# Two of four token tiles written in the output's order ahead of a feed-forward layer, their rows normalised there, and every result stored straight to the output

## The chip, the cores and the metric

The kernel runs on one core of one Trainium2 chip. The metric is device time of one execution in microseconds (us); a kernel's time is the median of its runs. The engines named below are TensorE (PE in the profile, PEld for its weight loads), VectorE (DVE), ScalarE (ACT), GpSimd (POOL) and SyncE (SP), whose queue issues the DMA transfers of this kernel.

## The reference

Eight batches, each of 448 tokens with 12 heads of 64 (768 channels), go through attention, a two-dimensional Fourier transform of which the real part is kept, a layer norm and a feed-forward layer.

```
q_n, k_n = rmsnorm(q, g_q), rmsnorm(k, g_k)
attn = softmax(q_n @ k_n^T / 8) @ v                # [8, 12, 448, 64]
x    = attn as [8, 448, 768]
u    = x + real(fft(fft(x, tokens), channels))
un   = (u - mean(u)) / sqrt(var(u) + 1e-6)
out  = u + relu(un @ w1) @ w2                      # 768 -> 3072 -> 768
```

All of it is wanted in fp32 accuracy. The kernel gets it by splitting each operand of a product into a high and a low part and multiplying in three passes.

## The kernel before, in words

**Stages.** For each batch there are two streams of work. `aux(b)` does the attention and the spectral part and ends in four token tiles: tiles of 113, 112, 111 and 112 rows (`LENS`) with 768 channels. Tiles 0 and 1 hold the first 225 tokens in descending order (they read `xT[:, :, 222 + t :: -2]`), tiles 2 and 3 (`mirror`) the rest. `ffn(b)` does the feed-forward layer of one batch: `up(m)` (18 matmuls, L866) makes one of 24 blocks of 128 hidden channels, `down(g, d)` (12 matmuls, L887) adds a group of four hidden blocks to one of six blocks `acc[:, d]` of output channels. Batch 0's `aux` runs first, with part of batch 1's; after that the driver merges `ffn(b)` with `aux(b+1)`, step by step in proportion to their costs, so that the last token tiles of `aux(b+1)` fall into the end of `ffn(b)`. The order of the instructions on each engine is then set by a scheduler that works on the merged list, and a change of one instruction can move its neighbours. The order of SP's DMA issues is set in the same way, and one that has to wait holds up those behind it.

**A token tile** (`token_tile`, L558 to L609). PE transposes x into PSUM (L578); two operations on DVE add the Fourier part, giving `u` and its row sums in `st`. SP stores `u` to a scratch in DRAM, `u_dram` (L591), from where it comes back later as the residual. DVE makes minus the mean from the row sums; ACT makes `un = u - mean` (Identity with a bias) and then squares `un` **into u**, with the row sums kept. This square overwrites `u`, so it waits until the L591 store has been read and has landed. DVE turns the sum into variance plus epsilon, GpSimd raises it to the power -1/2, and that is `rstd`. In the kernel before nothing ahead of the feed-forward layer uses `rstd`: since relu(r x) = r relu(x) for r > 0, the rows are scaled only at the output. In the profile the helpers' operations all carry L113.

**The feed-forward's input** (`ffn_input`, L773 to L789). For each of six blocks of 128 channels PE transposes the four tiles' pieces into one PSUM tile (24 transposes, L778); ACT copies it to `unT`'s high part and DVE subtracts to get the low part, 128 x 448 each.

**Weights.** They are converted in batch 0 (GpSimd, ACT and DVE; loads at L667, results to DRAM at L716) and afterwards loaded from there, once for each batch: a load is issued (L726) as soon as a matmul group has freed a buffer. w1 comes in tiles of 768 KB, w2 in tiles of 512 KB, three buffers each.

**The output** (`output_half` L823 to L841, `store` L804 to L819). The residual of a tile is loaded from `u_dram` (L828; rows of 113 and 111 go in two pieces), PE transposes three blocks of `acc` (L832), and DVE makes `rstd * product + residual`. A tile 2 or 3 is stored straight to every second row of the output (L819). For tiles 0 and 1, whose rows stand in descending order, the result is first stored to the scratch (L809) and then copied DRAM to DRAM with the rows reversed (L810), in pieces of 48 channels (192 bytes); token 224 goes by itself (L815). The output of batch b is done in the first `up` steps of batch b+1. In the last batch it is done in two halves of 384 channels, the second at the very end, with pieces of 24 channels.

## Time and profile before

| | |
|---|---|
| time, median of 3 runs | 2231.12 us (2229.54 to 2231.13) |
| span of the profiled execution | 2227.2 us |
| time of the profiled execution beyond its span | not given; the span is 3.9 us below the median |
| TensorE busy | 2092.4 us, 94% of the span |
| VectorE, ScalarE, GpSimd busy | 72%, 48%, 24% |
| feed-forward of batch 0 begins | 194.6 us |
| first residual load of batch 0's output | 517.4 us |

Rows of the profile are read as follows. A row of the timeline gives the start in us from the span's start, the duration, engine, line, operation and tiles (out<-in), a count when several like instructions are merged, and in brackets how long the engine had been idle and what released it. `SPq` rows are DMA issues: their duration is that of the issue, not that of the transfer, and where a row merges several (x3) it reaches from the first to the end of the last. A DMA row of the form "x1, 512.0 KB, 5.7" gives the issues in a window, their size and the median time from issue to landing. The windows view gives, for each stretch, its length, the busy time of PE, PEld, DVE, ACT and POOL with counts, the TensorE clock granted, the mean busy share of the DMA engines and GB/s. The view of one tile lists the forms of its operations with least, median and longest duration in ns.

### The profile page before, as it was taken

How to read it: one execution, taken by the hardware profiler on the slowest of the kernel's cores; microseconds unless marked ns; L12 is line 12 of the kernel's file. 1: busy time of each engine (PE TensorE's matmuls, PEld its weight loads, DVE VectorE, ACT ScalarE, POOL GpSimd, SP SyncE). 2: the span in 40 equal slices, each digit the busy share in tenths (PEclk: the TensorE clock that was granted, in tenths of full speed). 3: DMA queues.
4: the chain of work that ended last, by engine and by line, in shares of the span. 5: the costliest groups of instructions: out<-in, count | busy, mean ns of one | idle time of the engine just before them, and what ended most of it. 6: DMA issues, size and time to landing. Idle time of an engine off the chain costs nothing.

```text
span 2227.2 us, 31403 instructions
## 1 busy us (share of the span) xinstructions
PE 2092.4 (94%) x11164; PEld 1847.3 (83%) x11164; DVE 1612.1 (72%) x3083; ACT 1060.8 (48%) x2290; POOL 536.6 (24%) x322
## 2 busy tenths in 40 slices
PE   6877978779999999999999999999999999999997
PEld 3336867668999999999999999999999999998996
DVE  7897889788788587866787587867787687763122
ACT  6866766545554355524554355524554355422100
POOL 5773567644121021111211021101221022000000
PEclk8988988889999999999999999999999999999999
DMA  5555565658656675557655675558556674549665
GB/s 155 160 172 199 188 192 192 233 197 271 192 169 183 201 215 167 177 178 230 185 168 178 207 216 168 173 173 240 179 166 182 201 224 152 181 136 280 213 209 137
DMA packets 298238, 425.32 MB, mean 191 GB/s; under 512 B 186545, under 2 KB 224418, under 8 KB 298082
## 3 DMA queue, kind: packets, MB, share of 16 engines
q1 hardware_dynamic: 298082, 423.32, 61.1%
q8 instruction: 89, 1.46, 0.3%
q14 instruction: 67, 0.55, 0.1%
HBM read 363.47 MB, written 65.27 MB: 193 GB/s over the span
## 4 chain that ended last, share of the span: by engine, by line
PE 77%; DVE 10%; DMA 4%; ACT 4%; issue 2%; POOL 2%; SPq 0%; DVEq 0%; POOLq 0%; ACTq 0%
PE h L866 29%; PE o L887 27%; PE S L357 6%; PE av L443 4%; PE pt L431 4%; DMA dblw<-w 2%; PE y L546 1%; PE qk L320 1%; POOL magw L684 1%; DVE mn L113 1%; ACT P L113 1%; DMA w<-w 1%; DVE sm L113 1%; DVE eo L113 1%; PE oT L832 1%
## 5 line engine op out<-in xcount | busy, mean ns | idle before, releaser
L887 PE MATMUL o<-hs,w 128*128 128x448 f32 x3456 | 795.9, 371 | 11.5 <-DMA w<-w 4.4
L866 PE MATMUL h<-unT,w 128*128 128x448 f32 x3456 | 787.5, 373 | 7.5 <-ACT w L685 6.3
L866 PEld LDWEIGHTS h<-unT,w 128*128 128x128 f32 x3456 | 646.7, 190 | 61.3 <-ACT w L685 7.1
L887 PEld LDWEIGHTS o<-hs,w 128*128 128x128 f32 x3456 | 639.4, 189 | 68.1 <-issue 6.0
L113 ACT ACTIVATE P<-S,mn 112x448 f32<-112x448 f32 x384 | 243.3, 635 | 222.2 <-DVE mn L113 211.4
L113 DVE TENSOR_REDUCE mn<-S 112x1 f32<-112x448 f32 x384 | 233.7, 618 | 47.0 <-PE S L357 43.9
L113 POOL TENSOR_TENSOR qkn<-raw 112x1024 f32<-112x1024 f32 x47 | 90.3, 1922 | 719.7 <-PE qk L320 493.5
L113 ACT ACTIVATE hs<-h 128x448 fp32r<-128x448 f32 x192 | 104.4, 544 | 295.4 <-PE h L866 294.3
L113 DVE TENSOR_TENSOR acc<-o,acc 128x448 f32<-128x448 f32 x240 | 149.0, 621 | 109.8 <-PE o L887 108.5
L113 DVE SCALAR_TENSOR_TENSOR hs<-h,hs 128x448 fp32r<-128x448 f32 x192 | 119.2, 621 | 126.6 <-ACT hs L113 124.6
L113 ACT CAST T<-pt 128x448 fp32r<-128x448 f32 x252 | 133.0, 533 | 136.4 <-PE pt L431 134.2
L443 PE MATMUL av<-T,vhl 128*128 128x448 f32 x504 | 178.9, 387 | 13.2 <-DVE T L113 9.6
L113 DVE TENSOR_TENSOR T<-pt,T 128x448 fp32r<-128x448 f32 x252 | 154.9, 618 | 27.9 <-ACT T L113 26.2
L113 POOL TENSOR_TENSOR ss<-ss,nhalf 112x16 f32<-112x16 f32 x48 | 147.5, 3074 | 110.4 <-DVE ss L113 107.9
L113 DVE TENSOR_SCALAR P<-P,sm 112x448 f32<-112x448 f32 x336 | 164.9, 525 | 4.7
L431 PE MATMUL pt<-ident,P 112*128 112x112 f32 x1008 | 146.6, 263 | 8.2 <-ACT P L113 4.3
L357 PE MATMUL S<-KD,QT 128*112 128x448 f32 x352 | 138.8, 396 | 9.3 <-ACT P L113 4.8
L431 PEld LDWEIGHTS pt<-ident,P 112*128 112x128 f32 x1008 | 122.8, 143 | 28.6 <-ACT P L113 4.7
L113 POOL TENSOR_TENSOR rstd<-st,nhalf 112x1 f32<-112x1 f32 (+2 forms) x32 | 18.3, 572 | 494.8 <-DVE st L113 487.4
L357 PE MATMUL S<-rounded,QT 128*112 128x448 f32 x352 | 132.2, 377 | 1.7 <-DVE rounded L113 1.6
L443 PEld LDWEIGHTS av<-T,vhl 128*128 128x128 f32 x504 | 95.5, 190 | 24.7 <-DVE T L113 11.4
L113 DVE TENSOR_SCALAR sm<-sm 112x2 f32<-112x2 f32 x192 | 60.3, 314 | 59.0 <-ACT P L113 56.6
(122 smaller groups left out, 2598.8 us busy)
## 6 DMA issues: line engine op xcount, KB each, us to landing
w<-w SPq DMA_DIRECT2D x288, 512.0 KB, 4.4
w<-w SPq DMA_DIRECT2D x192, 768.0 KB, 4.6
dblw<-w SPq DMA_DIRECT2D x30, 512.0 KB, 4.3
dblw<-w SPq DMA_DIRECT2D x16, 768.0 KB, 4.4
raw<-q SPq DMA_DIRECT2D x96, 112.0 KB, 4.5
raw<-k SPq DMA_DIRECT2D x96, 112.0 KB, 3.4
v<-v SPq DMA_DIRECT2D x96, 96.0 KB, 3.5
u_dram<-u SPq DMA_DIRECT2D x24, 336.0 KB, 3.2
```

What stands on the lines that cost most here:

```text
L113: ins = emit(*args, **kwargs)
L320: nc.tensor.transpose(pt[:, c * C : (c + 1) * C], qk[:, i, c].rearrange("t h d -> t (h d)"), ident[:C, :C],)
L357: ins = nc.tensor.matmul(s_, QT[:, h, cs], K[:, h], start=step == 0, stop=step == 1)
L431: nc.tensor.transpose(pt[:, c * C : (c + 1) * C], Pc[c][:, 512 * h + j * 128 : 512 * h + (j + 1) * 128], ident[:C, :C],)
L443: nc.tensor.matmul(av[:, :S], lv, T[:, i], start=(j == 0 and i == 0), stop=False)
L546: nc.tensor.matmul(o, src[:, par, t0 : t0 + n], D1[:, ri, par, cols], start=i != 1, stop=i != 0,)
L684: behind(nc.gpsimd.tensor_tensor(out=bits, in0=bits, in1=low, op=ALU.add))
L832: nc.tensor.transpose(op[:n, j * 128 : (j + 1) * 128], accs[b][:, 3 * half + j, t0 : t0 + n], ident,)
L866: pace(nc.tensor.matmul(o, w[:, a, c], unT[c][:, z], start=n == 0, stop=n == 17))
L887: pace(nc.tensor.matmul(o, w[:, a, f], hs[4 * g + f][:, z], start=n == 0, stop=n == 11))
```

## The change

Four edits belong together:

- In `token_tile`, the tiles 0 and 1 get a further DMA behind the L591 store: a copy DRAM to DRAM with reversed rows from `u_dram` to a new scratch `u_turned` (L593), in pieces of 48 channels.
- The norm is finished there: ACT squares `u` with the bias directly (its result goes to `un`'s place and is not used), DVE and GpSimd make the reciprocal deviation, one more DVE operation makes the bias times it, and ACT writes the fully scaled `un`. `rstd` and its use at the output are gone.
- `ffn_input` writes the first 225 columns of each `unT` in reversed order: the copy by ACT and the subtraction by DVE are made in two pieces (225 and 223 columns), six more operations on each of the two engines for each batch.
- At the output the residual of tiles 0 and 1 is loaded from `u_turned`, DVE's operation is a plain addition, and all results are stored directly (L824, and L820 for token 224). The scratch store and the copy behind it (L809, L810) are gone: 18 of each before, against 16 copies at L593 now.

```diff
+TURNED = (N2, 0, NT, NT + N1 - 2)
...
             for r in rows_of(n):
                 nc.sync.dma_start(u_dram[b % 2, i4, r], u[r])
+            if not mirror:
+                nc.sync.dma_start(
+                    u_turned[b % 2, t, :n].rearrange("t (c d) -> c t d", c=16),
+                    u_dram[b % 2, t, n - 1 :: -1].rearrange(
+                        "t (c d) -> c t d", c=16
+                    ),
+                )
...
-            A.activation(un, u, AF.Identity, bias=st[:n, 2:3])
-            A.activation(u, un, AF.Square, accum_out=st[:n, 3:4])
-            rstd = sb.tile([N1, 1], F32, tag="rstd", name=f"rstd{b}_{i4}", bufs=8)
+            A.activation(un, u, AF.Square, bias=st[:n, 2:3], accum_out=st[:n, 3:4])
             V.tensor_scalar(
                 out=st[:n, 3:4], in0=st[:n, 3:4], scalar1=1.0 / DM, scalar2=EPS,
                 op0=ALU.mult, op1=ALU.add,
             )
             G.tensor_tensor(
-                out=rstd[:n], in0=st[:n, 3:4], in1=nhalf[:n, :1], op=ALU.pow
-            )
...
+                out=st[:n, 3:4], in0=st[:n, 3:4], in1=nhalf[:n, :1], op=ALU.pow
+            )
+            V.tensor_tensor(
+                out=st[:n, 2:3], in0=st[:n, 2:3], in1=st[:n, 3:4], op=ALU.mult
+            )
+            A.activation(
+                un, u, AF.Identity, bias=st[:n, 2:3], scale=st[:n, 3:4]
+            )
...
-            A.copy(t[:, 0], pt[:, :S])
-            sub(t[:, 1], pt[:, :S], t[:, 0])
+            for to, src in (
+                (t[:, :, :NT], pt[:, NT - 1 :: -1]), (t[:, :, NT:], pt[:, NT:S])
+            ):
+                A.copy(to[:, 0], src)
+                sub(to[:, 1], src, to[:, 0])
...
-        if i < 2:
-            turned = u_dram[b % 2, i]
-            nc.sync.dma_start(turned[:N2, cols], u[:N2, cols])
-            nc.sync.dma_start(
-                out[b, i : i + 223 : 2, cols].rearrange("t (c d) -> c t d", c=16),
-                turned[N2 - 1 :: -1, cols].rearrange("t (c d) -> c t d", c=16),
-            )
-            if i == 0:
-                nc.sync.dma_start(out[b, 224:225, cols], u[N2:n, cols])
...
+        if i == 0:
+            nc.sync.dma_start(out[b, 224:225, cols], u[:1, cols])
+            u, n = u[1:], n - 1
+        rows = out[b, i : i + 2 * n - 1 : 2] if i < 2 else out[b, 228 - i : S : 2]
+        for r in rows_of(n):
+            nc.sync.dma_start(rows[r, cols], u[r, cols])
...
+            kept = (u_turned if i < 2 else u_dram)[b % 2, i]
             for r in rows_of(n):
-                nc.sync.dma_start(residual[i][r], u_dram[b % 2, i, r])
+                nc.sync.dma_start(residual[i][r], kept[r])
...
-        V.scalar_tensor_tensor(
-            out=uh, in0=op[:n, :384], scalar=rstds[b, i][:n], in1=uh,
-            op0=ALU.mult, op1=ALU.add,
-        )
+        add(uh, op[:n, :384], uh)
```

SP's queue at the end of batch 2's feed-forward, where the last token tiles of batch 3 are made, reads as follows before the change. `u_1` and `u_3` are the odd token tiles, `w_105` to `w_107` w2 tiles of 512 KB, and `ur_0` is the residual of batch 2's tile 0.

```order
L726 DMA w_105_9706<-w_5_108 128x1024
L591 DMA u_dram<-u_1_9530 112x768
L726 DMA w_106_9722<-w_5_108 128x1024
L591 DMA u_dram<-u_3_9552 112x768
L828 DMA ur_0_9837<-u_dram 112x768
L828 DMA ur_0_9837<-u_dram 1x768
L726 DMA w_107_9738<-w_5_108 128x1024
```

The same place after the change:

```order
L735 DMA w_105_9747<-w_5_109 128x1024
L591 DMA u_dram<-u_1_9570 112x768
L735 DMA w_106_9763<-w_5_109 128x1024
L593 DMA u_turned<-u_dram 16x112x48
L591 DMA u_dram<-u_3_9593 112x768
L834 DMA ur_0_9890<-u_turned 112x768
L834 DMA ur_0_9890<-u_turned 1x768
L735 DMA w_107_9779<-w_5_109 128x1024
```

The reversed copy of tile 1 now stands between the weight load `w_106` and the store of `u_3`, ahead of the weight load `w_107`; it reads what the `u_1` store two places before it writes. The pattern is the same in each of the five transitions to batches 2 to 6.

On DVE, at the same place of the program, the two operations that make `u_1` stand among the reductions of the attention (`mn`, the row extremes of the scores) and the additions to `acc`. Before:

```order
L113 TENSOR_REDUCE mn_0_0_9878<-S_0_0_0_9880 112x1
L113 SCALAR_TENSOR_TENSOR u_1_9530,st_1_9531<-x_100_9534,smdf_1_9511 112x384
L113 SCALAR_TENSOR_TENSOR u_1_9530,st_1_9531<-x_101_9539,smdf_1_9511 112x384
L113 TENSOR_REDUCE mn_0_0_9878<-S_0_0_1_9881 112x1
L113 TENSOR_TENSOR acc_7236<-o_5_0_9692,acc_7236 128x448
```

After:

```order
L114 TENSOR_REDUCE mn_0_0_9930<-S_0_0_0_9932 112x1
L114 TENSOR_REDUCE mn_0_0_9930<-S_0_0_1_9933 112x1
L114 SCALAR_TENSOR_TENSOR u_1_9570,st_1_9571<-x_100_9574,smdf_1_9551 112x384
L114 SCALAR_TENSOR_TENSOR u_1_9570,st_1_9571<-x_101_9579,smdf_1_9551 112x384
L114 TENSOR_TENSOR acc_7277<-o_5_0_9733,acc_7277 128x448
```

The second reduction has moved ahead of `u_1`.

At the end of the program SP's queue holds the second half of the last batch's results. Its last eight transfers before the change:

```order
L809 DMA u_dram<-ur_0_21335 112x384
L815 DMA out_dram<-ur_0_21335 1x384
L809 DMA u_dram<-ur_1_21346 112x384
L819 DMA out_dram<-ur_3_21365 112x384
L810 DMA out_dram<-u_dram 16x112x24
L819 DMA out_dram<-ur_2_21355 96x384
L810 DMA out_dram<-u_dram 16x112x24
L819 DMA out_dram<-ur_2_21355 15x384
```

And its last six after it:

```order
L824 DMA out_dram<-ur_0_21434 112x384
L824 DMA out_dram<-ur_1_21444 112x384
L824 DMA out_dram<-ur_2_21452 96x384
L824 DMA out_dram<-ur_3_21462 112x384
L824 DMA out_dram<-ur_2_21452 15x384
L820 DMA out_dram<-ur_0_21434 1x384
```

The two stores to the scratch and the two copies that read it are replaced by two direct stores.

More of the change, by code (lines that the diff above doesn't have):

```diff
@@ L185, in spectral_block @@
     u_dram = dram.tile([2, 4, N1, DM], F32, name="u_dram")
+    u_turned = dram.tile([2, 2, N1, DM], F32, name="u_turned")
     def load_gains():
@@ L485, in attention @@
             yield 0
-    rstds = {}
     halves = {}
@@ L604, in token_tile @@
             G.tensor_tensor(
-                out=rstd[:n], in0=st[:n, 3:4], in1=nhalf[:n, :1], op=ALU.pow
+                out=st[:n, 3:4], in0=st[:n, 3:4], in1=nhalf[:n, :1], op=ALU.pow
             )
-            rstds[b, i4] = rstd
-            u = un
-            uns[i4] = u
+            V.tensor_tensor(
[4 more added lines that the diff above has]
+            )
+            uns[i4] = un
         for t in range(2):
@@ L806, in store @@
         cols = slice(0, DM) if half is None else slice(half * 384, half * 384 + 384)
-        if i < 2:
-            turned = u_dram[b % 2, i]
-            nc.sync.dma_start(turned[:N2, cols], u[:N2, cols])
-            nc.sync.dma_start(
-                out[b, i : i + 223 : 2, cols].rearrange("t (c d) -> c t d", c=16),
-                turned[N2 - 1 :: -1, cols].rearrange("t (c d) -> c t d", c=16),
-            )
-            if i == 0:
-                nc.sync.dma_start(out[b, 224:225, cols], u[N2:n, cols])
-        else:
-            rows = out[b, 228 - i : S : 2, cols]
-            for r in rows_of(n):
-                nc.sync.dma_start(rows[r], u[r, cols])
+        if i == 0:
[4 more added lines that the diff above has]
+            nc.sync.dma_start(rows[r, cols], u[r, cols])
     residual = {}
     def output_half(b, i, half, tag):
-        n, t0 = LENS[i], OFFS[i]
+        n, t0 = LENS[i], TURNED[i]
         if half == 0:
             residual[i] = slot("P", f"ur{b}_{i}")[:, :DM]
+            kept = (u_turned if i < 2 else u_dram)[b % 2, i]
             for r in rows_of(n):
-                nc.sync.dma_start(residual[i][r], u_dram[b % 2, i, r])
+                nc.sync.dma_start(residual[i][r], kept[r])
         u = residual[i]
```

## The prediction

> **What bounds the kernel now.** I read first the head of the page, then the table by stretches, then what PE waits for, then the places that the change touches.
>
> ```profile
> span 2227.2 us, 31403 instructions
> PE 2092.4 (94%) x11164; PEld 1847.3 (83%) x11164; DVE 1612.1 (72%) x3083; ACT 1060.8 (48%) x2290; POOL 536.6 (24%) x322
> ```
>
> ```profile
> core 0: us, PE busy (x) PEld busy (x) DVE busy (x) ACT busy (x) POOL busy (x), PEclk, DMA share, GB/s
> 181.00:198.00 17.00, 8.57 (x42) 7.19 (x42) 13.38 (x35) 13.35 (x23) 7.53 (x6) 0.68 0.55 189
> 198.00:260.00 62.00, 62.00 (x332) 56.34 (x332) 45.73 (x84) 44.62 (x94) 28.07 (x19) 0.98 0.65 207
> 260.00:320.00 60.00, 47.48 (x229) 39.92 (x228) 53.83 (x90) 40.20 (x82) 39.57 (x24) 0.89 0.60 195
> 780.00:1029.00 249.00, 249.00 (x1395) 228.59 (x1394) 188.06 (x382) 116.92 (x262) 39.30 (x22) 1.00 0.62 189
> 2204.00:2227.00 23.00, 10.08 (x61) 9.14 (x58) 6.79 (x12) 0.00 (x0) 0.00 (x0) 0.81 0.60 125
> ```
>
> From 780 to 1029 us, one whole batch, PE has no gap at all, while DVE is busy for 188 of 249 us and ACT for 117. What PE waits for outside batch 0 is short:
>
> ```profile
> PE o L887 <- DMA w<-w: 4.4, 3, 2.3
> ```
>
> So an edit counts only where it reaches PE: in the end of the program after PE's last matmul (10.08 us busy of the last 23), in batch 0 (PE idle for 8 of 17 us and 12 of 60 us in the two quoted stretches), and wherever a weight load, the thing PE does wait for, becomes late.
>
> **The end of the program: a gain.** The last results leave DVE and go through SP as follows.
>
> ```profile
> 2213.79 2.19 DVE L113 SCALAR_TENSOR_TENSOR ur<-oT,rstd,ur 113x384 f32<-113x384 f32 x4 [0.46 <-PE oT L832]
> ```
>
> ```profile
> 2215.29 0.31 SPq L809 DMA_DIRECT2D u_dram<-ur  x1
> 2216.01 0.32 SPq L819 DMA_DIRECT2D out_dram<-ur  x1
> 2218.62 0.56 SPq L810 DMA_DIRECT2D out_dram<-u_dram  x1
> ...
> 2220.25 0.56 SPq L810 DMA_DIRECT2D out_dram<-u_dram  x1
> ```
>
> ```profile
> out_dram<-u_dram SPq DMA_DIRECT2D x1, 168.0 KB, 5.4
> u_dram<-ur SPq DMA_DIRECT2D x2, 168.0 KB, 3.7
> ```
>
> The second copy is issued at 2220.25 and lands 5.4 us later, at 2225.65; the span ends 1.55 us behind that. Afterwards four large stores go out as DVE finishes, the last at about 2216.0 as now (DVE ends at 2215.98), and two short ones of one and 15 rows behind it, 0.3 us of issue each (the row at 2215.29), so the queue ends at 2216.6. A direct store has no row of this size and moment; its nearest rows are the scratch stores L809 of the same 168 KB, 3.7 us here, and 2.9 over all four of this size:
>
> ```profile
> u_dram<-ur SPq DMA_DIRECT2D x4, 168.0 KB, 2.9
> ```
>
> Landing lies between 2216.0 + 2.9 - 0.7 = 2218.2 (half-empty rings, since no copy of small pieces is under way) and 2216.6 + 3.7 + 0.2 = 2220.5; I take 2219.1, near the median of four. That is **-6.5 us** (-5.2 to -7.5).
>
> **The five transitions to batches 2 to 6: a loss.** There the new copy L593 has to wait for the landing of the store that it reads, and SP's queue stands still behind it. Behind it are the store of `u_3`, the two residual loads, and a weight load that PE will need. This is the queue before, in the transition to batch 3, with the ACT operation that waits for the same landing, and the matmuls that need the weights:
>
> ```profile
> 1017.31 0.38 SPq L591 DMA_DIRECT2D u_dram<-u  x1
> 1019.32 0.32 SPq L726 DMA_DIRECT2D w<-w  x1
> 1020.93 0.32 SPq L591 DMA_DIRECT2D u_dram<-u  x1
> 1021.34 0.71 SPq L828 DMA_DIRECT2D ur<-u_dram  x2
> 1022.42 6.50 SPq L726 DMA_DIRECT2D w<-w  x3
> ```
>
> ```profile
> 1022.88 0.85 ACT L113 ACTIVATE u<-un 112x768 f32<-112x768 f32 x1 [3.62 <-DMA u_dram<-u]
> ```
>
> ```profile
> w<-w SPq DMA_DIRECT2D x1, 512.0 KB, 5.7
> ```
>
> ```profile
> 1029.31 2.58 PE L887 MATMUL o<-hs,w 128*128 128x448 f32 x12
> ```
>
> The load issued at 1022.42 lands at 1028.1 and is needed at 1029.31: 1.2 us to spare. The store issued at 1017.31 has landed only at 1022.88, as ACT's wait shows, 5.6 us later, since weight loads fill the rings. L593 can be issued then, and costs 0.60 us of SP's time:
>
> ```profile
> L810 SPq DMA_DIRECT2D out_dram<-u_dram x18: 555/603/1737, 547.0 to 2220.2; - x18
> ```
>
> Behind it come 0.32 (store), 0.09 (the gap between 1021.25 and 1021.34) and 0.71 (two residual loads): 1022.88 + 1.72 = 1024.60, so the load goes out 2.2 us later than now (the gap of 0.37 us ahead of it today is a wait that is over by then). PE waits 2.2 - 1.2 = **1.0 us**. The transition to batch 5 gives less:
>
> ```profile
> 1520.74 0.84 ACT L113 ACTIVATE u<-un 112x768 f32<-112x768 f32 x1 [2.55 <-DMA u_dram<-u]
> 1520.82 6.50 SPq L726 DMA_DIRECT2D w<-w  x3
> 1527.72 2.58 PE L887 MATMUL o<-hs,w 128*128 128x448 f32 x12
> ```
>
> With the same 5.7 us (the row of that window reads alike) the load has 1.2 us to spare, and goes out at 1520.74 + 1.72 = 1522.46, 1.6 us later: PE waits 0.4 us. The mean of 0.7 over five transitions is 3.5 us. Two further shares come on top. First, the order on DVE puts one more reduction ahead of `u_1`:
>
> ```profile
> 1017.02 0.62 DVE L113 TENSOR_REDUCE mn<-S 112x1 f32<-112x448 f32 x1
> ```
>
> With the spare time already used up, its 0.6 us count in full, 5 x 0.6 = 3.0. Second, the copy itself runs in the rings beside the weight load. No row shows that pair; from below it costs nothing, from above it costs the load what a copy of small pieces takes beyond a plain store, 5.4 - 2.9 = 2.5 us. I take 0.3, near the bottom, since a whole weight load of 512 KB takes 5.7 us and the copy's 336 KB are spread over the same engines with other waiting stores and loads between: 5 x 0.3 = 1.5. Together **+8 us**; from below 3 (if the landing comes early and only `u_1`'s shift is left), from above 3.5 + 3.0 + 12.5 = 19.
>
> By the Trainium skill, page "DMA: Bandwidth & Descriptors", section "Queues, rings and completion order", each DMA engine consumes the descriptors of one ring in ring order, so a load issued behind the copy starts on each engine only after the copy's share there. By that rule the term would stand at its upper end; it is the third rival below. The 5.6 us that a plain store took here behind weight loads speak for the rule, without separating it from mere sharing.
>
> **The other transitions.** The copies of tile 0 come earlier in the queue, with no load near its limit behind them. The last transition, to batch 7, is late already:
>
> ```profile
> 2020.87 2.68 PE L887 MATMUL o<-hs,w 128*128 128x448 f32 x12 [2.31 <-DMA w<-w]
> ```
>
> ```profile
> L591 SPq DMA_DIRECT2D u_dram<-u x48: 278/320/436, 178.6 to 2012.3; - x48
> ```
>
> There a token tile's store is far ahead (the last L591 is issued at 2012.3), so the copy's wait can fall into time that SP has; **0** (-2 to +3, the size of the wait itself).
>
> **The start of batch 0's feed-forward: a small loss.** Its first matmul stands here:
>
> ```profile
> 194.56 0.74 PE L866 MATMUL h<-unT,w 128*128 128x448 f32 x1 [0.38 <-DVE magw L672]
> ```
>
> Before, `un` needs one ACT pass behind the mean. Afterwards it needs the square, the read of its sum, one operation on DVE, one on GpSimd, one more on DVE, and then the pass:
>
> ```profile
> L113 DVE TENSOR_SCALAR st<-st x64: 141/180/217, 179.0 to 2016.2; 112x1 f32<-112x1 f32 x32, 113x1 f32<-113x1 f32 x16, 111x1 f32<-111x1 f32 x16
> L113 POOL TENSOR_TENSOR rstd<-st,nhalf x32: 537/548/998, 182.8 to 2016.5; 112x1 f32<-112x1 f32 x16, 113x1 f32<-113x1 f32 x8, 111x1 f32<-111x1 f32 x8
> L113 ACT ACTIVATE u<-un x32: 834/846/852, 181.5 to 2015.2; 112x768 f32<-112x768 f32 x16, 113x768 f32<-113x768 f32 x8, 111x768 f32<-111x768 f32 x8
> L113 ACT ACTIVATION_READ_ACCUMULATOR u<-un x32: 183/186/192, 182.3 to 2016.0; 112x1 f32 x16, 113x1 f32 x8, 111x1 f32 x8
> ```
>
> That is 0.85 + 0.19 + 0.18 + 0.55 + 0.18 = 1.95 us more, and about 0.1 for each of four handoffs between engines (ACT's next pass at 1022.88 + 0.85 starts within 0.1): 2.3. PE is idle here for 8.4 of 17 us and then full until 260, so nearly all of it delays PE; behind 260 it idles again and can catch up a little. **+2 us** (0 to +3.5).
>
> **The rest of batch 0: 0 (-6 to +6.4).** Its conversions go through SP, which already waits, and the two new copies of batch 1's tiles add two more waits:
>
> ```profile
> SPq L667 <- POOL magw L684: 101.2, 36, 7.4
> u_dram<-u SPq DMA_DIRECT2D x24, 336.0 KB, 3.2
> ```
>
> Each is at most the landing of such a store, 3.2 us, so 6.4 in all. DVE is busy for 54 of 60 us from 260 to 320, so what the scheduler moves there can cost or gain as much; nothing tells the sign.
>
> **Costed at nothing.** In the steady stages ACT and DVE have room (117 and 188 of 249 us): that covers the two-piece copies of `unT` and DVE's extra product; the plain addition at the output changes no count. ACT's waits for stores go away,
>
> ```profile
>   ACT u L113: 39.7, 25
> ```
>
> but ACT is not what PE waits for, so 39.7 us of idle time are worth nothing. The longer chain of `un` at a transition is covered by `down` matmuls that PE does meanwhile; were that cover gone, it would cost 2.3 us at each of seven. The loss of 18 scratch stores and the copies at the output frees DMA time that is off PE's path.
>
> **The sum.** -6.5 + 8 + 0 + 2 + 0 = +3.5 on a span of 2227.2 gives 2230.7. The median of the runs lies 3.9 above the span, so the time is **2234.6 us**, 0.16% above the 2231.1 of before. About 0.2%, 4.5 us, is what a measurement can tell from no change, so this is a forecast of no change, on its slow side.
>
> **The rivals.** *Only the end counts.* The weight load need not be last: if stores land 1.2 us earlier than ACT's wait shows, or PE finds other matmuls to do first, the transitions and the start cost nothing, and 2227.2 - 6.5 + 3.9 = 2224.6, about 2225. For it speaks that the wait is only 0.4 to 1.0 us; against it that five transitions have the same order. Chance 0.24.
>
> *The conversions are stretched.* If both new waits of SP in batch 0 hold up conversions, 6.4 us are added to my sum: 2241. It decides once the queue at L667 is what DVE waits for; for it speaks that SP is held there for 101 us, against it that it is held by GpSimd, which stays late anyway. Chance 0.14.
>
> *The weight load waits for the whole copy.* Then each load is late by a further 2.5 us, the term is 19, and the time is 2227.2 - 6.5 + 19 + 2 + 3.9 = 2245.6, about 2246, slower. It decides as soon as the copy's pieces stand ahead of the load on every engine and are not worked off before the load is issued about 1.1 us later. For it speaks 5.4 against 2.9 us; against it that the load has 5.7 us in which the two can overlap. Chance 0.13.
>
> That the change takes the copies away is not so: 16 stand at L593 where 18 stood at L810; it moves them from the output to the token tiles.
>
> **How the numbers follow.** My forecast has 0.49; its own range is 2228.5 (transitions 3, the end -7.5) to 2240.5 (half of the 2.5 us at each load, 3.5 + 3.0 + 6.3 = 12.8, and the end -5.2). "Same" reaches from 2226.7 to 2235.6. Of my forecast's 0.49, 0.30 lie in it and 0.19 above; of the first rival 0.20 below and 0.04 in it; of the second 0.03 in it and 0.11 above; the third is all above. That makes faster 0.20, same 0.37, slower 0.43. The range of 2224.5 to 2245.0 takes in the forecast, the upper part of the first rival (0.15), the second and a third of the last.
>
> **What would show it.** In the profile of the changed kernel: a last store that lands about 2219 on the old scale; PE waits at L887 for a weight load at five transitions, 1 to 2 us each, with L593 ahead of that load in SP's queue; a first `up` matmul about 2 us later than 194.56; no ACT wait for `u_dram`. Wrong it would be if PE shows no such waits (then the first rival), if they are 3 us and more (the third), or if the feed-forward of batch 1 begins over 4 us off.

## The result and the profile after

The changed kernel takes 2253.47 us (median of 4 runs, 2252.97 to 2256.68) against 2231.12 (2229.54 to 2233.94): a ratio of 1.0104, 95% interval 1.0089 to 1.0119. It is 1% slower, 22 us, where 2234.6 and a range up to 2245 had been forecast; the highest of the rivals had 2246. The head of its page:

```profile
span 2254.7 us, 31515 instructions
PE 2109.9 (94%) x11164; PEld 1854.1 (82%) x11164; DVE 1617.0 (72%) x3163; ACT 1072.8 (48%) x2338; POOL 536.9 (24%) x322
```

The matmuls are the same in number; the span is 27.5 us longer. To see where, I took the start of the first `up` matmul of batches 0, 1 and 7, and the end of the last `down`, in both traces:

| place | before | after | later by |
|---|---|---|---|
| matmul S after the first `ab`, ahead of the first token tile | 175.6 | 178.8 | 3.2 |
| first `up`, batch 0 | 194.6 | 204.8 | 10.2 |
| first `up`, batch 1 | 537.4 | 559.6 | 22.2 |
| first `up`, batch 7 | 2031.8 | 2068.2 | 36.4 |
| last `down` ends | 2212.7 | 2247.5 | 34.8 |
| span | 2227.2 | 2254.7 | 27.5 |

The first 3.2 us are no effect of the change: up to there both kernels do the same in the same order. The windows view of before and then of after has, for 80 to 100 us,

```profile
80.00:100.00 20.00, 16.09 (x69) 6.35 (x68) 16.37 (x30) 15.83 (x40) 16.21 (x11) 1.00 0.54 175
```

```profile
80.00:100.00 20.00, 16.27 (x54) 6.02 (x54) 14.26 (x26) 13.66 (x35) 16.21 (x11) 0.78 0.44 142
```

The granted clock (the column behind POOL's count) is 1.00 in the one execution and 0.78 in the other, and 15 fewer matmuls were done in as much busy time. In the profiles of the other runs this place lies 1.2 to 4.6 us later than in that of before; I take it out of every comparison below. What is left: **start of batch 0's feed-forward +7.0, rest of batch 0's stage +11.9, the six transitions from there to batch 7 +14.3, the last feed-forward -1.6, the end -7.2**; sum 24.4 (the medians differ by 22.4). Forecast had been +2, 0, +8, 0 and -6.5. Each profile is one execution, and the one of before was a quick one: in the other runs the span lies 1.8 to 2.1 us below the time of the same execution, in before 3.9 us below the median. So whether a kernel as a whole is faster is read from the medians.

**The end** is as forecast. SP's queue of after, with the landing times of those of L824's stores that were traced (two, both in this last stretch of the program):

```profile
2249.16 2.54 SPq L824 DMA_DIRECT2D out_dram<-ur  x5
2251.75 0.24 SPq L820 DMA_DIRECT2D out_dram<-ur  x1
```

```profile
DMA to landing us min/median/max: 2.1/2.2/2.3
```

The queue is empty at 2252.0, and no issue waits for a landing any more.

**A transition**, that of batch 3, in SP's queue of after, with the weight load's landing and PE's row:

```profile
1039.48 0.32 SPq L591 DMA_DIRECT2D u_dram<-u  x1
1041.37 0.32 SPq L735 DMA_DIRECT2D w<-w  x1
1045.07 0.57 SPq L593 DMA_DIRECT2D u_turned<-u_dram  x1
1045.74 0.87 SPq L591 DMA_DIRECT2D u_dram<-u  x1
1046.69 0.84 SPq L834 DMA_DIRECT2D ur<-u_turned  x2
1047.62 0.85 SPq L735 DMA_DIRECT2D w<-w  x2
```

```profile
w<-w SPq DMA_DIRECT2D x1, 512.0 KB, 5.5
```

```profile
1053.28 2.67 PE L890 MATMUL o<-hs,w 128*128 128x448 f32 x12 [1.62 <-DMA w<-w]
```

What SP waited for ahead of L593, from 1039 to 1048 us, is the landing of that store:

```profile
SPq L593 <- DMA u_dram<-u: 3.3, 1, 3.3
```

L593 goes out 5.6 us after the store that it reads, and the weight load behind it lands at 1053.1, just ahead of the matmuls that wait for it: PE stood for 1.62 us where before it had 1.2 us in hand. From L593 to that load SP needs 2.55 us (2.6 to 3.0 at the other transitions), where 1.72 had been summed: the store between them is issued in 0.87 us and not in 0.32. Over all transitions PE now waits for

```profile
PE o L890 <- DMA w<-w: 10.2, 8, 3.2
PE h L869 <- DVE unT L114: 2.0, 2, 1.0
PE o L890 <- DVE unT L114: 1.4, 1, 1.4
PE qk L322 <- ACT P L114: 1.0, 2, 0.5
```

That is 14.6 us, against 4.4 us for weights at the same places before (all but 0.5 of it at the transition to batch 7). By transition, to batches 2 to 7, the loss is -0.1, 2.1, 3.6, 2.4, 6.0 and 0.3 us. That to batch 6 is the longest for one more reason: right behind the wait the granted clock fell, and twelve matmuls that took 2.58 us before took 4.24, as PE's row and the windows view show:

```profile
1811.13 4.24 PE L890 MATMUL o<-hs,w 128*128 128x448 f32 x12 [1.94 <-DMA w<-w]
```

```profile
1808.00:1816.00 8.00, 6.06 (x24) 5.18 (x24) 3.81 (x11) 3.30 (x12) 0.00 (x0) 0.79 0.58 197
```

The same happens at the transition to batch 7 (0.79 from 2056 to 2064 us). Before, the granted clock was 1.00 at both places.

**The start of the feed-forward.** ACT, GpSimd, DVE and PE of after, around the last token tile:

```profile
197.51 0.93 ACT L114 ACTIVATE un<-u,st 112x768 f32<-112x768 f32 x1
...
200.71 0.66 ACT L680 ACTIVATE dblw<-dblw 128x512 uint32<-128x512 uint32 x1 [1.25 <-DMA dblw<-w]
201.27 0.64 ACT L679 ACTIVATE magw<-dblw 128x512 f32<-128x512 f32 x1
201.81 1.01 ACT L114 ACTIVATE un<-u,st 112x768 f32<-112x768 f32 x1
```

```profile
197.68 1.80 POOL L695 TENSOR_TENSOR w1e<-magw1e,w1e 128x768 fp32r<-128x768 f32 x1 [0.53 <-ACT w1e L694]
199.45 0.54 POOL L114 TENSOR_TENSOR st<-st,nhalf 112x1 f32<-112x1 f32 x1
```

```profile
200.02 0.16 DVE L114 TENSOR_TENSOR st<-st 112x1 f32<-112x1 f32 x1 [1.30 <-POOL st L114]
```

```profile
204.76 0.74 PE L869 MATMUL h<-unT,w 128*128 128x448 f32 x1 [0.88 <-ACT unT L114]
```

The tile's square is summed at about 198.5, but GpSimd takes up its power only at 199.45, behind a conversion's operation of 1.80 us, and ACT its last pass only at 201.81, behind two operations of a conversion of which the first waited for its load. The chain crosses the queues of three engines that also hold conversions, and waits in two of them: of the 4.3 us from the sum of the square to the end of the last pass, 1.9 are work and 2.4 waiting.

**The stretch between the first `up` of batch 0 and that of batch 1**, before and after, in the windows view (columns as in the prediction):

```profile
194.60:537.40 342.80, 281.36 (x1382) 244.53 (x1383) 293.91 (x481) 217.84 (x422) 192.92 (x122) 0.89 0.64 215
```

```profile
204.80:559.60 354.80, 289.44 (x1395) 248.21 (x1396) 306.04 (x511) 221.11 (x435) 198.79 (x123) 0.89 0.63 207
```

DVE is the busiest engine in this stage, 86% of it before, and it is busy for 12 us more: in the new order more of batch 2's attention stands ahead of the last weight conversion. PE is busy for 8 us more. SP's wait for the landing that the new copy needs is short in this stretch:

```profile
SPq L593 <- DMA u_dram<-u: 1.9, 1, 1.9
```

### The profile page after: what moved, and what is told of

It is laid out like the page before. It is cut to its first block, busy times and chain, and to the rows that moved or that the text cites. A ratio compares the mean times of both kernels' runs of the same rounds, so it can differ in the third digit from the quotient of the medians.

```text
span 2254.7 us, 31515 instructions
## 1 busy us (share of the span) xinstructions
PE 2109.9 (94%) x11164; PEld 1854.1 (82%) x11164; DVE 1617.0 (72%) x3163; ACT 1072.8 (48%) x2338; POOL 536.9 (24%) x322
## 4 chain that ended last, share of the span: by engine, by line
PE 75%; DVE 11%; DMA 4%; issue 4%; ACT 4%; POOL 2%; SPq 0%; POOLq 0%; DVEq 0%; ACTq 0%
PE h L869 28%; PE o L890 26%; PE S L359 5%; PE av L445 4%; PE pt L433 4%; DMA dblw<-w 2%; DMA w<-w 2%; DVE mn L114 2%; PE y L546 1%; DVE P L114 1%; ACT P L114 1%; PE qk L322 1%; DVE sm L114 1%; POOL magw L693 1%; DVE eo L114 1%
## 5 line engine op out<-in xcount | busy, mean ns | idle before, releaser
L890 PE MATMUL o<-hs,w 128*128 128x448 f32 x3456 | 798.9, 373 | 22.5 <-DMA w<-w 10.2
L445 PE MATMUL av<-T,vhl 128*128 128x448 f32 x504 | 184.3, 395 | 16.3 <-DVE T L114 8.7
L114 POOL TENSOR_TENSOR st<-st,nhalf 112x1 f32<-112x1 f32 (+2 forms) x32 | 18.2, 568 | 466.0 <-DVE st L114 465.8
L114 ACT ACTIVATE un<-u,st 112x768 f32<-112x768 f32 (+2 forms) x64 | 62.2, 980 | 71.4 <-DVE st L114 71.4
```

Source lines behind the costliest of these rows:

```text
L114: ins = emit(*args, **kwargs)
L445: nc.tensor.matmul(av[:, :S], lv, T[:, i], start=(j == 0 and i == 0), stop=False)
L890: pace(nc.tensor.matmul(o, w[:, a, f], hs[4 * g + f][:, z], start=n == 0, stop=n == 11))
```

## The experiments

All but three were built from one source in which the two halves of the change can be chosen by batch: `TURN` (reversed copies, two-piece reversed input, direct stores) and `NORM` (rows scaled ahead of the feed-forward). With both empty it is the kernel before, with both `range(8)` the changed one. The other three, before_r47, before_r44 and after_r44, are the kernel before and the changed kernel with one number changed.

| run | time | ratio, 95% interval | start | batch 0 | transitions | last ffn | end |
|---|---|---|---|---|---|---|---|
| changed kernel | 2253.47 | 1.0104 (1.0089 to 1.0119) | 7.0 | 11.9 | 14.3 | -1.6 | -7.2 |
| late | 2241.14 | 1.0041 (1.0026 to 1.0056) | 0.1 | 3.0 | 17.0 | -0.3 | -7.3 |
| early_norm | 2243.94 | 1.0048 (1.0032 to 1.0065) | 7.5 | 8.2 | 0.9 | 1.4 | -0.3 |
| early_turn | 2251.57 | 1.0082 (1.0067 to 1.0097) | 1.3 | 20.6 | -4.3 | -1.0 | -0.2 |
| last_turn | 2226.03 | 0.9972 (0.9962 to 0.9981) | 0.3 | 0.2 | 0.9 | 0.6 | -6.3 |
| before_r47 | 2244.64 | 1.0052 (1.0037 to 1.0067) | 0.1 | 14.6 | -1.9 | 0.6 | -0.2 |
| after_r44 | 2255.31 | 1.0103 (1.0077 to 1.0128) | 7.3 | 11.7 | 19.9 | -1.9 | -7.5 |
| late_moved | 2242.57 | 1.0045 (1.0029 to 1.0060) | 0.0 | -0.2 | 18.2 | -0.5 | -7.2 |
| late_turn | 2240.58 | 1.0037 (1.0023 to 1.0050) | 0.0 | -0.2 | 14.9 | 0.1 | -6.3 |
| late_held | 2234.53 | 1.0016 (1.0007 to 1.0025) | 0.6 | 1.8 | 3.9 | 6.3 | -7.2 |
| held_turn | 2229.95 | 0.9996 (0.9986 to 1.0006) | 0.1 | 0.1 | 2.2 | 4.6 | -6.8 |
| late_norm | 2229.04 | 0.9998 (0.9987 to 1.0009) | 0.2 | -1.7 | -0.5 | 0.3 | -1.2 |
| early_split | 2244.77 | 1.0068 (1.0053 to 1.0083) | 0.8 | 13.3 | -1.9 | 0.4 | -0.5 |
| before_r44 | 2245.38 | 1.0051 (1.0036 to 1.0066) | 0.4 | 12.8 | 1.6 | 0.4 | -0.5 |
| split_r43 | 2241.54 | 1.0038 (1.0024 to 1.0052) | 1.5 | 8.6 | 1.0 | -0.2 | -0.2 |
| early_copy | 2242.85 | 1.0038 (1.0023 to 1.0053) | 0.1 | 15.2 | -2.9 | -0.8 | -0.2 |
| late_mix | 2229.33 | 0.9982 (0.9972 to 0.9991) | 0.3 | 3.6 | 2.5 | 0.3 | -6.9 |

The times are medians; the ratios are to the kernel before on the same chip, whose median was between 2230.7 and 2233.5 us in the four sets of runs. The other columns come from the one profiled execution: us later than in the kernel before, of the places in the table above, taken as differences (from matmul S to the first `up` of batch 0, to that of batch 1, to that of batch 7, to the last `down`, to the end).

How finely these columns can be read is shown by eight of the runs (late, last_turn, late_moved, late_turn, late_held, held_turn, late_norm, late_mix). Their edits begin with batch 2 or later, and up to the first `up` of batch 1 PE, DVE, ACT and GpSimd do the same operations in the same order as in the kernel before. Their start column still lies between 0.0 and 0.6 us, and their batch 0 column between -1.7 and 3.6: differences of that size in batch 0 are scatter between executions.

**late: the change without batches 0 and 1.**

```diff
+TURN = NORM = range(2, 8)
```

> The whole change, but only for batches 2 to 7; batches 0 and 1 are as in the kernel before. Theory A (the loss sits in two stages: about 19 us in the stage to the end of batch 0's feed-forward, about 15 us at the transitions to batches 3 to 7, against a gain of 7 us at the end): the stage to the first matmul of batch 1's feed-forward stays at 537 us, the transitions cost some 13 to 15 us and the end gains 7: 2237 to 2240 us. Rival B (what is lost later is only an effect of a stage that began late, or of that one execution): the transitions cost under 4 us and the kernel is at 2224 to 2228 us.

Measured: 2241.14 us, transitions 17.0, the end -7.3. Theory A holds: the loss is not of one place, and the transitions lose on a kernel that was on time before them. Without the transition to batch 2, which the forecast did not count and which lost 2.6 us, the 17.0 are 14.4, within the 13 to 15 forecast.

**early_norm and early_turn: each half, in batches 0 and 1 only.**

```diff
+TURN, NORM = (), (0, 1)
```

> Only the norm's edit, only for batches 0 and 1: rows fully normalised ahead of the feed-forward, nothing reversed, the output's path as before. Theory N (the longer chain through ACT, DVE and GpSimd ahead of batch 0's feed-forward and the work that it moves make the loss of batch 0): the first matmul of the feed-forward at about 201 us (194.6 before), batch 1's feed-forward some 15 to 19 us later than 537 us, and 2246 to 2250 us in all. Theory Q (SP's waits for the reversed copies make it): 2231 to 2234 us, only the 2 us of the start.

```diff
+TURN, NORM = (0, 1), ()
```

> Only the turning, only for batches 0 and 1: the reversed copies on SP, the two-piece copies of the feed-forward's input and the direct stores, with the norm finished at the output as before. Theory Q (SP's waits hold up the conversions' loads in batch 0): batch 1's feed-forward 15 to 19 us later than 537 us, 2246 to 2252 us in all. Theory N (the norm's chain makes it): the first matmul of the feed-forward near 195 us, batch 1's feed-forward within 4 us of 537 us, 2230 to 2236 us.

Measured: both lose, 8.2 us and 20.6 us behind the start, where together they lose 11.9. Each half loses what the theory that blames it had forecast or more, so neither theory, which clears the other half, stands: what loses is not one of the edits, and the losses don't add up. (Where batch 0's stage takes in more of batch 2's attention, the transition to batch 2 is shorter, by 2.7 us in early_turn: that much of its 20.6 is most likely work done early.) Only the start is plain: 7.5 us with the norm's edit and 1.3 without.

**last_turn: the turning for the last batch only.**

```diff
+TURN, NORM = (7,), ()
```

> Only the turning, only for the last batch, with the norm finished at the output as before. Theory A (the gain at the end is whole, and the last transition costs about 1 us): 2224 to 2225 us, 0.3% faster. Rival B (the reversed copies hold up a weight load at the last transition, where PE waits already, and take the gain back): 2228 to 2232 us.

Measured: 2226.03 us, 0.28% faster (0.19 to 0.38%), the end -6.3, all six transitions 0.9. Theory A holds, and this version beats both kernels.

**before_r47, after_r44, before_r44: the order alone.** `RATIO_FIRST` sets how much of batch 1's and 2's `aux` is merged into batch 0's feed-forward.

```diff
-RATIO_FIRST = 0.45
+RATIO_FIRST = 0.47
```

> The kernel before with one number changed, RATIO_FIRST 0.47 for 0.45: the same work, none of the change's edits, but on DVE four row reductions, four scalings of P and two subtractions of QT of batch 2's attention and two of batch 1's unT stand ahead of the last weight conversion, nearly as in the changed kernel. Theory D (batch 0's loss behind its first matmul is work that DVE, which bounds that stage, does before the last conversions): batch 1's feed-forward begins 7 to 14 us later than 537 us and the time is 2238 to 2246 us. Rival Q (the loss comes from SP's waits for the copies): no more than 2 us either way, 2230 to 2235 us.

```diff
-RATIO_FIRST = 0.45
+RATIO_FIRST = 0.44
```

> The whole change with one number changed, RATIO_FIRST 0.44 for 0.45: on DVE no reduction of batch 2's scores stands ahead of the last weight conversion any more than in the kernel before. Theory D: the stretch from the first matmul of batch 0's feed-forward to that of batch 1's falls from 355 us to 343 to 347 us, and the time from 2253 to 2241 to 2246 us. Rival Q: the stretch stays within 3 us of 355 us, 2250 to 2256 us.

> The kernel before with one number changed, RATIO_FIRST 0.44 for 0.45: the same work, and on DVE a little less of batch 2's work ahead of the last weight conversion than in the kernel before (one reduction, two scalings, three subtractions of unT fewer). Theory D (the loss grows with the work that DVE has ahead of the last conversion): batch 1's feed-forward begins 0 to 4 us earlier, 2226 to 2232 us. Theory N (the order of batch 0's stage stands at a narrow optimum, and a shift to either side loses): 5 to 14 us later, 2236 to 2246 us.

The windows view of batch 0's stretch, in before_r47 and then in before_r44:

```profile
196.90:554.40 357.50, 292.30 (x1397) 251.22 (x1398) 301.15 (x500) 223.54 (x432) 201.01 (x125) 0.88 0.62 208
```

```profile
196.20:551.90 355.70, 286.01 (x1383) 247.46 (x1384) 299.66 (x480) 218.96 (x421) 195.86 (x122) 0.89 0.62 208
```

Before_r47 does none of the change's edits and loses 14.6 us in batch 0's stage, more than the changed kernel does there (11.9). That fits theory D. But after_r44, which takes batch 2's reductions away from ahead of the last conversion, gains nothing (11.7), and before_r44, shifted to the other side, with 480 instructions of DVE in the stretch where before has 481, loses 12.8. Theory D falls; theory N, a narrow optimum, fits all three.

What the time goes into differs. For DVE's operations in this stretch I took the shortest duration of each form, and called what an operation takes beyond it stretching: the stretch before is 63.3 us of stretching, 230.6 of other busy time (own work) and 48.9 idle. The changed kernel has +7.1, +4.9 and 0.0; before_r47 +7.5, -0.2 and +7.4; before_r44 -0.4, +5.9 and +7.3.

**early_split, split_r43, early_copy: single edits in batch 0's stage.** The first two split the copies of `unT`, in natural order:

```diff
-            A.copy(t[:, 0], pt[:, :S])
-            sub(t[:, 1], pt[:, :S], t[:, 0])
+            for to, src in (
+                (t[:, :, :NT], pt[:, :NT]), (t[:, :, NT:], pt[:, NT:S])
+            ) if b < 2 else ((t, pt[:, :S]),):
+                A.copy(to[:, 0], src)
+                sub(to[:, 1], src, to[:, 0])
```

> The kernel before with nothing but the two-piece copies of the feed-forward's input for batches 0 and 1, not reversed (225 and 223 columns, the same values at the same places): no reversed copy on SP, no change of the norm. On DVE four reductions, two or three scalings and two subtractions of QT come to stand ahead of the last weight conversion, as in the changed kernel. Theory D (the order on DVE in batch 0's stage makes the loss): batch 1's feed-forward 8 to 15 us late, 2239 to 2247 us. Rival Q (the copies on SP make it): within 3 us, 2230 to 2235 us.

```diff
-RATIO_FIRST = 0.45
+RATIO_FIRST = 0.43
```

> The run named early_split (two-piece copies for batches 0 and 1 and nothing else) with RATIO_FIRST 0.43: no reduction of batch 2's scores ahead of the last conversion any more than in the kernel before. Theory D: the loss of 14 us goes down to 0 to 4 us, 2231 to 2236 us. Theory N: 6 to 14 us of it stay, 2237 to 2246 us.

The third has only the copies to a scratch:

```diff
+            if not mirror and b < 2:
+                nc.sync.dma_start(
+                    u_turned[b % 2, t, :n].rearrange("t (c d) -> c t d", c=16),
...
```

> The kernel before with nothing but the reversed copies of batches 0 and 1, into a scratch that nobody reads; input and output as before. On DVE three reductions and two subtractions of QT of batch 2 and two of batch 1's unT come to stand ahead of the last conversion. Theory D or N (any shift of the order in batch 0's stage): batch 1's feed-forward 5 to 14 us late, 2236 to 2246 us. Theory Q (only SP's waits for the landing of two stores count): 0 to 6.4 us, 2231 to 2238 us.

Measured: 13.3, 8.6 and 15.2 us in batch 0's stage. Splitting two batches' copies, with no SP wait and no column more to work on, costs as much there as the whole change; shifting its order back regains a third of it. The copies that nobody reads, two of them in this stage, cost 15.2, more than twice what SP could wait for them by the forecast (6.4). SP's wait for them from 198 to 556 us was

```profile
SPq L597 <- DMA u_dram<-u: 5.1, 2, 4.0
```

So theory Q falls as well: even if all of it counted, two thirds of the loss would be left, and early_split, before_r47 and before_r44 lose without any such wait.

**late_moved: a miss.** The copies were written into the middle of the feed-forward.

```diff
             hs[m] = t
             W1.load()
+            if m in (8, 12) and b in TURN:
+                t, n = m // 4 - 2, LENS[m // 4 - 2]
+                nc.sync.dma_start(
+                    u_turned[b % 2, t, :n].rearrange("t (c d) -> c t d", c=16),
...
```

> The whole change for batches 2 to 7 as in the run named late, but the reversed copies are issued in the middle of that batch's own feed-forward, when the stores that they read have long landed, so that SP waits for nothing. Theory W (SP's wait ahead of a weight load makes the transitions' cost): all of the 17 us of the six transitions go, PE has no wait at them beyond those of the kernel before, 2225 to 2228 us. Rival C (the longer chain of the norm makes it, and PE then waits for unT): under 5 us of it go, 2236 to 2241 us.

Measured: transitions 18.2, as in late. This says nothing on theory W. SP's queue at batch 3's transition shows why:

```profile
1026.54 0.57 SPq L911 DMA_DIRECT2D u_turned<-u_dram  x1
1027.21 1.13 SPq L595 DMA_DIRECT2D u_dram<-u  x1
1028.43 0.73 SPq L854 DMA_DIRECT2D ur<-u_turned  x2
1029.25 1.25 SPq L745 DMA_DIRECT2D w<-w  x2
```

The scheduler had put the copy (L911 here) back to where its store is, since nothing tied it to the place where it was written.

**late_turn, late_norm: each half, in batches 2 to 7.**

```diff
+TURN, NORM = range(2, 8), ()
```

> The turning alone for batches 2 to 7, copies in their place behind the stores, with the norm finished at the output as before. Theory W: the transitions cost what they did in the run named late, some 2.5 us each, and PE waits there for a weight load; 2237 to 2241 us. Rival C: the transitions cost under 1 us each, 2225 to 2229 us.

```diff
+TURN, NORM = (), range(2, 8)
```

> The norm's edit alone for batches 2 to 7, nothing turned, the output's copies as before. Theory B or C: PE waits 1 to 2 us for unT at each transition, 8 to 14 us in six, no gain at the end: 2239 to 2246 us. Theory W: under 3 us in six, 2231 to 2235 us.

Measured: 14.9 us at the transitions with the turning alone, -0.5 with the norm alone. PE's waits for weights from 560 to 2020 us in late_turn and then in late_norm, and its waits at L923 in late:

```profile
PE o L923 <- DMA w<-w: 7.3, 6, 2.4
```

```profile
PE o L923 <- DMA w<-w: 0.6, 1, 0.6
```

```profile
PE o L923 <- DVE unT L116: 4.8, 3, 1.9
PE o L923 <- DMA w<-w: 3.9, 3, 2.0
```

The norm's longer chain is covered at the transitions, as forecast. In late the first row names `unT` at every second transition. There the weight load had been issued 5.55 us before PE went on, as in this row and PE's row of the same transition:

```profile
1286.36 8.57 SPq L752 DMA_DIRECT2D w<-w  x4
```

```profile
1291.91 1.46 PE L923 MATMUL o<-hs,w 128*128 128x448 f32 x6 [1.25 <-DVE unT L116]
```

That is what such a load takes (5.6 to 5.9 us in the transitions of before), and late_norm has no such wait: the releaser named is most likely not the last one.

**late_held, held_turn, late_mix: the copy out of the way.** Now each copy is tied behind a matmul in the middle of the feed-forward, in the order only.

```diff
+                order(
+                    nc.sync.dma_start(
+                        u_turned[b % 2, t, :n].rearrange("t (c d) -> c t d", c=16),
...
+                    ),
+                    paced[-1], mybir.DependencyClass.Sync, mybir.DependencyReason.SCHED_ONLY,
+                )
```

Late_held has this tie with a data dependency in place of the last argument and both halves of the change, held_turn the turning only; in late_mix batch 7's copies stay behind their stores.

> The whole change for batches 2 to 7, with the reversed copies tied behind a matmul in the middle of that batch's own feed-forward, so that in SP's queue they really stand there (in the run named late_moved they had been put back behind the stores) and no weight load at a transition is behind such a wait. Theory W (SP's wait makes the transitions' cost): the six transitions cost under 3 us together instead of 17, 2226 to 2229 us. Theory C (the norm's chain makes it): 13 to 17 us as before, PE waits for unT, 2238 to 2242 us. Theory B (both, each enough to stop PE in the same place, since both end in the same o matmuls): 8 to 14 us, the waits for unT stay and those for weights go at every second transition.

> The turning alone for batches 2 to 7, norm finished at the output, copies held in the middle of the feed-forward. What is left of the change at a transition is the two-piece copy of the feed-forward's input and the loads' changed places. Theory B: nothing left that stops PE, under 1 us for each transition, 2224 to 2227 us, as in the run named last_turn. Rival S (the two-piece reversed copies by themselves delay PE): 2 us for each transition, 2234 to 2238 us.

> The turning alone for batches 2 to 7, the copies of batches 2 to 6 held in the middle of their feed-forward and those of batch 7 in their place behind the stores, norm at the output. If the held copies of the last batch took the loss of 5 us inside that batch's feed-forward (its weight loads then follow each other without the other stream's work between): that loss goes and the gain at the end stays, 2223 to 2226 us. Rival: the loss inside the last feed-forward comes from the direct stores or residual loads of batch 6, and stays, 2228 to 2231 us.

SP's queue of late_held at batch 4's transition, and held_turn's waits of PE from 560 to 2020 us:

```profile
1276.56 0.32 SPq L595 DMA_DIRECT2D u_dram<-u  x1
1276.93 0.75 SPq L854 DMA_DIRECT2D ur<-u_turned  x2
1278.03 9.74 SPq L745 DMA_DIRECT2D w<-w  x4
```

```profile
PE o L927 <- DMA w<-w: 0.6, 2, 0.4
```

The transitions fall from 17.0 to 3.9 with both halves and from 14.9 to 2.2 with the turning alone; in held_turn all but 0.1 of the rest lies in the transition to batch 7, where PE waits for weights about as long as before (4.1 and 4.0 us) and the granted clock is 0.79 from 2024 to 2032 us, where it was 1.00. What late_held keeps lies in the transitions to batches 4 and 6, with a PE wait of 0.7 us for `unT` in each; late_norm and held_turn, each with one half, have no such wait. Theory W is shown for most of the cost: it is SP's wait ahead of the weight load. Tying the copy elsewhere also takes its traffic away from the load, but that is not what cost the time: behind the copy, in the transitions to batches 2 to 6 of all runs that have it there, the twelve traced loads took 5.1 to 7.0 us (5.8 in the mean), and the 42 traced without it, in the other runs, 5.4 to 6.6 (5.9).

As a whole neither reaches its forecast: late_held is 0.16% slower than the kernel before and held_turn as fast (0.9996). Inside the last feed-forward held_turn loses 4.6 us, where PE waits for weights,

```profile
PE o L927 <- DMA w<-w: 3.2, 2, 3.1
```

and late_held 6.3. With batch 7's copies back in their place (late_mix) the last feed-forward loses 0.3: it was the held copies that stood in that batch's way. Late_mix as a whole is 0.18% faster (0.09 to 0.28%), 4.2 us by the medians, less than forecast; why is not shown. The 3.6 us in its batch 0 column are within the scatter named above.

## Why the prediction was wrong, point by point

- **What bounds the kernel:** right. PE's busy time bounds all but batch 0 and the end, and only edits that reach PE counted.
- **The end, -6.5:** right, -7.2 (-6.3 with the turning alone). Direct stores landed in about 2.2 us. The 2.9 that the forecast took for four scratch stores is the mean of the two that were traced, 2.2 and 3.7, and the 0.7 us taken off at its lower bound stood in no row; the direct stores landed like the quicker one.
- **The transitions, +8 (3 to 19):** the mechanism was right, SP's wait for a landing ahead of a weight load, and the sum, 14.3 in the changed kernel, lies in the range. At the row where it was worked out PE waited 1.62 us where 1.0 and the shift of 0.6 had been forecast; that is in part luck, since SP's own time behind the wait was 2.55 us and not 1.72. Four of the five transitions forecast lost, 2.1 to 6.0 us each where 1.6 had been summed, and that to batch 2 lost nothing. Left out of the sum were the longer time of SP, waits for `unT` and for the attention's `P`, 1.0 and 0.5 us early in the feed-forwards of batches 3 and 5 ("covered", the forecast had said), and the fall of the granted clock behind two of the waits.
- **The third rival** (each load late by a further 2.5 us, a price taken from the rows of 5.4 and 2.9) does not describe this: the load behind the copy took 5.5 us at both transitions of the changed kernel where it was traced, the one before the change 5.7. By the Trainium skill, "DMA: Bandwidth & Descriptors", section "Queues, rings and completion order", each engine takes up the descriptors of a ring in order. The load goes out about 2.5 us or more after the copy, so runs here cannot say what a load directly behind it would take.
- **The start, +2 (0 to 3.5):** failed in size, +7.0, and early_norm (7.5) shows that it comes with the norm's edit. The step summed the added operations' durations and 0.1 us for each handoff. ACT, DVE and GpSimd take their operations in the order of their queues, with conversions between; behind GpSimd's 1.80 us and ACT's two conversion operations the last tile waited longer than it was worked on.
- **The rest of batch 0, 0 (-6 to +6.4):** this is the step that failed. Its words were "what the scheduler moves there can cost or gain as much; nothing tells the sign", and only SP's two waits had a price. It is +11.9, of which SP's wait can be 1.9. Nine kernels with another order in batch 0, seven of them without the whole change, lose 8 to 21 us there; the eight with the order of before lie between -1.7 and 3.6. Two of the nine (before_r47, before_r44) shift the same work to either side of the present order, with none of the change's edits, and lose 14.6 and 12.8. So what had no price is the new order itself: each of the nine that were tried is a loss. Before these runs nothing on record told that sign. Of the forecast's own signs of being wrong this is the one that came: batch 1's feed-forward began more than 4 us off.
- **The sum.** Measured and forecast differ by 20.9 us on the profile: 11.9 in the rest of batch 0, 6.3 at the transitions, 5.0 at the start, -1.6 in the last feed-forward and -0.7 at the end.
- **What stays open:** why the present order is so much better than its neighbours. DVE has more work ahead of the last conversion in some runs, stretched operations or idle time in others. Much of the loss is there when the conversions are done: counted from batch 0's first `up`, DVE's last operation on one ends 4.2 to 13.0 us later than before in the nine, and -1.6 to 3.6 in the eight. A kernel with all of the change and precisely the old order in batch 0 was not tried, so that the changed kernel's own 11.9 us come from the order is argued from these neighbours.

## What to carry to other kernels

An edit in a stage that several in-order engines share nearly fully is priced by running the old work in a slightly other order first: if that alone loses 13 us, as here on both sides, an edit that moves the scheduler there must be expected to lose as much. A DMA that has to wait for another's landing belongs where nothing urgent is queued behind it, and it had to be tied there, since this scheduler put it back to its producer. Of a change with a gain in one place and costs in others, try that place alone: the turning for the last batch keeps 6 of the 7 us at the end, and its median is 6.8 us below that of the kernel before.

## What the runs showed of the hardware

DVE's operations can take many times their own duration. In batch 0's stage of the changed kernel 62 of them took over 0.3 us more than the shortest of their form, 61.0 us together, and each of the 62 ran beside operations of GpSimd for at least as long as its excess. DVE's and then GpSimd's rows around one of them:

```profile
310.23 2.33 DVE L114 TENSOR_SCALAR sm<-sm 112x2 f32<-112x2 f32 x1
312.59 0.17 DVE L114 RECIPROCAL sm<-sm 112x2 f32<-112x2 f32 x1
312.79 1.25 DVE L114 TENSOR_SCALAR P<-P,sm 112x448 f32<-112x448 f32 x1
```

```profile
308.95 2.34 POOL L114 TENSOR_TENSOR qkn<-raw 112x1024 f32<-112x1024 f32 x1
311.25 1.28 POOL L114 TENSOR_TENSOR vhl<-v,vhl 128x512 fp32r<-128x512 f32 x1
312.49 1.30 POOL L693 TENSOR_TENSOR magw<-magw,dblw 128x512 uint32<-128x512 uint32 x1
```

A scaling of two columns takes 2.33 us (0.15 at its shortest) and ends as GpSimd's second operation does, at 312.5. The Trainium skill, "SBUF — State Buffer", section "SBUF: two separate sides", says that a VectorE operation in a two-port mode, or with two inputs in SBUF against a GpSimd operation that reads there, and one of GpSimd take a shared pair of ports as an exclusive lock for a whole instruction, and that the later one waits; these rows agree. So how long DVE takes for a given work depends on what stands beside it on GpSimd, 55 us of such excess in this stage before the change and 61 after: one way in which a new order can cost time without new work.

And the clock granted in the first 150 us differs between executions of the same instructions: 1.2 to 4.6 us lie there between the profile of before and those of the other runs. Behind a wait of PE it can fall too, as shown at 1811 us of the changed kernel, but it did not behind the 1.62 us at 1053; what decides is not shown.
